# Narrowing the first layer's weights with Prelu, the first batch on small array tiles, and a new issue order

## The chip, the cores and the metric

The kernel runs on one core of a Trainium2 chip. Its metric is the device time of one execution in microseconds (us); lower is better. The profile shows one execution, taken by the hardware profiler. Engines are named as the profile names them: PE multiplies matrices (PEld loads its weights), DVE is the vector engine, ACT the scalar engine, POOL GpSimd, and SP issues the DMAs.

## What is computed

The inputs are float32, except that the four weight matrices reach the device as float64 words. A state attends to tokens and tokens to the state, in both directions; the two results, 2176 tokens of width 512, go through two feed-forward layers.

```python
B, H, S, Ns, D = (4, 8, 512, 32, 64)
a = softmax(scale * x @ state.T)          # per batch and head, over the 32 states
xread = a @ state
a2 = softmax(scale * state @ x.T)         # over the 512 tokens
sread = a2 @ x
x = concatenate([xread, sread])           # 4 * (512 + 32) tokens of 512
h = x @ w_in                              # 512 -> 1024
solu = h * softmax(h)
ln = (solu - mean(solu)) / sqrt(var(solu) + 1e-6) * g_ln
x = ln @ w_out                            # 1024 -> 512
h = x @ w2_in                             # 512 -> 2048
out = (h * tanh(softplus(h))) @ w2_out    # 2048 -> 512
```

## The kernel before

The 2176 tokens are 17 tiles of 128: four of each batch's 512 tokens, and tile 16 with the states of all four batches. Three stages follow each other, without a barrier between them.

**Start.** `s_load_w_in` and `s_load_w_out` (L275, L287) bring eight pieces each of the first layer's two weight matrices, 128x512 words of 64 bits, 512 KB apiece. `narrow` (L146) turns a piece into float32 with integer steps on the upper and the lower 32-bit word. It multiplies the upper word, read as a float32, by 2 to the power -112 (on ACT, L155, or on DVE, L153, as the flag string `W` says); it brings the lower word's top bits into place (ACT L158 or DVE L160, flag `B`); it shifts the upper word left by 3 and joins the two (DVE L165). The shift drops the sign. Either a second DVE instruction puts it back (L169), or, where flag `T` is 1, ACT has first written a float16 copy of the upper word over its upper half, which carries the sign to where the shift keeps it (L163). `s_gw` (L298) then splits each piece of `w_out`, scaled by `g_ln`, into a high part on ACT (L305) and a rest on DVE (L307).

The first batch's attention stands apart from that of the others. Its state is loaded as a block diagonal `bd_t` of 128x64 for each pair of heads; `s_tok_scores` (L321) and `s_tok_exp` (L329) compute the token side with the tokens on the partitions, `s_scores0` (L374) the state side with one matmul for a pair of heads, and `s_sw0` (L508) the product of state and `w_in`, one matmul for a pair and a half, which needs two of the eight pieces of `w_in` at a time. The other batches use `s_scores` and `s_sw` (L381, L518), eight matmuls each on tiles of 64 rows by 32 columns of the array, which write 32-partition strips of one PSUM tile; a half of `s_sw` needs four of the pieces of `w_in`. `s_back` (L451) weighs the tokens by the state's softmax, for the first batch with 64-column matmuls (L463), for the others with 32-column ones (L470).

**First layer.** For each tile `s_a0` (L529) makes `h` with matmuls of `aT` and `sw` (L548), `s_a1` (L553) the softmax and the normalisation (its first instruction is the maximum on DVE, L557), `s_turn` or `s_turn_far` the transpose, and `s_d` (L629) the product with `gw` (L640).

**Second layer.** Three passes over eight blocks (L868 on): `s_hp` (L884) multiplies with `w2_in` by a Strassen scheme of seven products, `s_post` combines them on DVE (the first of these combinations is L898), `s_act` applies Mish, `s_po` and `s_block` multiply with `w2_out`. The second layer's weights come and are narrowed (by the same `narrow`, with n of 16 and above) in the first pass.

`s_warm` (L240) issues matmuls on a constant tile, 26 at first and then groups of 4 where the flag string `R` has a 0; nobody reads their result.

The order of all of this is written out: each step is a generator, `ORDER` is a string of step numbers, two characters each, and the loop at L1174 advances the step named next by one `yield`. Each engine works in the order in which its instructions were so issued, and SP issues the DMAs in that order too. The flag strings choose the engine of single instructions.

## Time and profile before

| | us |
|---|---|
| median of 3 runs | 571.43 |
| lowest and highest | 570.12, 571.88 |
| the profiled execution's own time | 570.37 |
| its span in the profile | 568.6 |

In the span PE is busy for 98%, DVE for 89%, ACT for 63% and POOL for 9%. The busy share of an engine is a mean over stages with different limits, so the views below are cut by time. "Idle before" is the time for which an engine had nothing running just ahead of an instruction, with what ended it. A row with xN merges N instructions that follow each other.

### The profile page before, as it was taken

The numbers are of one execution on the slowest core, as the hardware profiler recorded it, in microseconds if no ns is written. First come the engines' busy times: TensorE is split into PE (matmuls) and PEld (weight loads), VectorE is DVE, ScalarE is ACT, GpSimd is POOL, SyncE is SP. The second block draws the span as 40 slices with busy tenths as digits, with TensorE's granted clock in tenths as the row PEclk, the third lists the DMA queues.
The fourth block names the chain that finished last, engine by engine and source line by source line (L and its number), as shares of the span: only waits on it lengthen the run. The fifth ranks groups of instructions, "written<-read, shape, count | busy, mean of one in ns | idle before, by whom it ended". The sixth has DMA issues, their size and how long they took to land. (4 is left out here: it accounts for less than half of the span.)

```text
span 568.6 us, 9811 instructions
## 1 busy us (share of the span) xinstructions
PE 555.6 (98%) x3513; PEld 491.9 (87%) x3513; DVE 504.5 (89%) x964; ACT 358.4 (63%) x660; POOL 52.2 (9%) x128
## 2 busy tenths in 40 slices
PE   9899999999999998999999999999999999999997
PEld 3434788899699997888988899999999999999996
DVE  5999989995779879999999998398999999998995
ACT  5998968565468646999979774643334635443340
POOL 0102212120023000000000000000000034000023
PEclk9999999999999999999999999999999999999999
DMA  8963225054217979999897979785796669897932
GB/s 307 415 229 113 75 88 185 27 174 124 75 75 221 300 254 325 316 329 343 310 336 297 355 277 382 273 302 203 249 338 235 253 222 345 282 342 279 318 125 94
DMA packets 50016, 139.19 MB, mean 245 GB/s; under 512 B 5680, under 2 KB 22704, under 8 KB 49968
## 3 DMA queue, kind: packets, MB, share of 16 engines
q1 hardware_dynamic: 49968, 138.57, 68.7%
q8 instruction: 28, 0.46, 0.3%
q14 instruction: 20, 0.16, 0.1%
HBM read 98.18 MB, written 40.37 MB: 244 GB/s over the span
## 5 line engine op out<-in xcount | busy, mean ns | idle before, releaser
L884 PE MATMUL hp<-xo,w2r 128*128 128x384 f32 (+1 forms) x504 | 93.8, 329 | 0.4 <-ACT w2r L705 0.3
L884 PEld LDWEIGHTS hp<-xo,w2r 128*128 128x128 f32 x504 | 84.5, 188 | 3.5 <-ACT w2r L705 0.7
L884 PE MATMUL hp<-xo,w2swh 128*128 128x384 f32 (+1 forms) x336 | 82.9, 330 | 3.1 <-DVE m L895 1.0
L640 PE MATMUL pm<-ln_l,gw_hi 128*128 128x256 f32 (+1 forms) x256 | 76.8, 300 | 0.0
L640 PE MATMUL pm<-ln_h,gw_hi 128*128 128x256 f32 (+1 forms) x256 | 75.0, 293 | 0.0
L640 PE MATMUL pm<-ln_h,gw_lo 128*128 128x256 f32 (+1 forms) x256 | 74.5, 291 | 0.0
L996 DVE TENSOR_TENSOR acc<-po,acc 128x384 f32<-128x384 f32 (+1 forms) x136 | 69.0, 521 | 2.6 <-PE po L991 1.6
L884 PEld LDWEIGHTS hp<-xo,w2swh 128*128 128x128 f32 x336 | 59.1, 188 | 6.4 <-DVE m L895 1.3
L925 ACT ACTIVATE gh<-c 128x384 fp32r<-128x384 f32 (+1 forms) x57 | 29.3, 516 | 51.8 <-DVE c L906 44.9
L884 PE MATMUL hp<-xo,w2swl 128*128 128x384 f32 (+1 forms) x168 | 55.1, 328 | 0.0
L963 ACT CAST qh<-t 128x384 fp32r<-128x384 f32 (+1 forms) x60 | 28.9, 489 | 37.1 <-DVE t L955 22.5
L640 PEld LDWEIGHTS pm<-ln_l,gw_hi 128*128 128x128 f32 x256 | 48.2, 188 | 3.0 <-issue 1.6
L640 PEld LDWEIGHTS pm<-ln_h,gw_hi 128*128 128x128 f32 x256 | 48.2, 188 | 1.2 <-issue 0.7
L640 PEld LDWEIGHTS pm<-ln_h,gw_lo 128*128 128x128 f32 x256 | 48.7, 190 | 0.0
L906 DVE TENSOR_TENSOR c<-hp,u 128x384 f32<-128x384 f32 (+1 forms) x72 | 38.1, 531 | 10.7 <-PE hp L884 9.9
L548 PE MATMUL ph<-swh,aT 128*128 128x512 f32 x128 | 44.1, 449 | 0.4 <-ACT ph L566 0.4
L989 PE MATMUL po<-ql,w2oh 128*128 128x384 f32 (+1 forms) x120 | 39.3, 328 | 0.2 <-DVE acc L996 0.2
L990 PE MATMUL po<-qh,w2oh 128*128 128x384 f32 (+1 forms) x120 | 38.7, 323 | 0.0
L991 PE MATMUL po<-qh,w2ol 128*128 128x384 f32 (+1 forms) x120 | 38.7, 323 | 0.0
L965 DVE TENSOR_TENSOR ql<-t,qh 128x384 fp32r<-128x384 f32 (+1 forms) x60 | 32.0, 544 | 0.6 <-ACT qh L963 0.2
L548 PEld LDWEIGHTS ph<-swh,aT 128*128 128x128 f32 x128 | 22.6, 189 | 10.7 <-issue 4.3
L884 PEld LDWEIGHTS hp<-xo,w2swl 128*128 128x128 f32 x168 | 31.5, 188 | 0.0
(454 smaller groups left out, 1346.5 us busy)
## 6 DMA issues: line engine op xcount, KB each, us to landing
w2r<-ki SPq DMA_DIRECT2D x16, 768.0 KB, 5.8
w2ol<-ko SPq DMA_DIRECT2D x15, 768.0 KB, 6.1
w2oh<-ko SPq DMA_DIRECT2D x15, 768.0 KB, 6.7
w<-in_w2i SPq DMA_DIRECT2D x16, 512.0 KB, 5.7
w2swh<-ki SPq DMA_DIRECT2D x8, 896.0 KB, 6.2
w2swl<-ki SPq DMA_DIRECT2D x8, 896.0 KB, 7.3
td<-tt SPq DMA_DIRECT2D x12, 512.0 KB, 2.7
ln_l<-td SPq DMA_DIRECT2D x48, 128.0 KB, 3.1
```

The costliest lines, as they stand in the source:

```text
L548: nc.tensor.matmul(out=ph[:, hf * 512:(hf + 1) * 512], lhsT=a_[:, c * P:(c + 1) * P], rhs=w_[:, q, hf * 512:(hf + 1) * 512], start=q == 0 ...
L640: nc.tensor.matmul(out=pm[:, :n], lhsT=w_[:, k, m * P:(m + 1) * P], rhs=l_[:, c0:c0 + 4 * len(blk), k, :], start=k == 0 and j == 0, stop=k ...
L884: nc.tensor.matmul(out=r, lhsT=w_[:, 0, k * P:(k + 1) * P], rhs=x_[:, k, :n], start=s in (0, 1, 3, 4) and cnt == 0, stop=cnt == 5, skip_gr ...
L906: nc.vector.tensor_tensor(out=c, in0=bank[ps, fp, s], in1=u, op=ALU.add)
L925: nc.scalar.activation(out=gh, in_=src, func=AF.Mish)
L963: nc.scalar.copy(out=hi, in_=src)
L965: on('V', ((ps - 1) * NFP + fp) * 4 + int(name[1]) - 1).tensor_tensor(out=lo, in0=src, in1=f32(hi), op=ALU.subtract)
L989: nc.tensor.matmul(out=r, lhsT=wh[:, a, c], rhs=x[1], start=first or not held, stop=False)
L990: nc.tensor.matmul(out=r, lhsT=wh[:, a, c], rhs=x[0], start=False, stop=False)
L991: nc.tensor.matmul(out=r, lhsT=wl[:, a, c], rhs=x[0], start=False, stop=last or not held)
L996: on.tensor_tensor(out=o, in0=x, in1=y, op=ALU.add)
```

## The change

`narrow` handles n below 16, the first layer's sixteen pieces, in a way of its own. The upper word goes through one ACT instruction, Prelu with a scale of 2 to the power -112 and a slope of 2 to the power 32 for negative values. A negative value comes out with 32 added to its exponent, and the shift by 3 moves that exponent bit into the sign's place. The lower word is treated as before, and one DVE instruction joins the two. The second DVE instruction, the float16 copy and the choice of the engine for the multiplication (flag `W`) are gone for these pieces.

The first batch's `s_scores0` and `s_sw0` are removed; `s_scores(0)` and `s_sw(0, hf)` take their place, and `s_back(0, q)` uses the code of the other batches. `s_tok_scores` keeps its matmuls and writes their 64 columns as two runs of 32.

`ORDER` is a new string (3144 entries in place of 3182), and nine flag strings have other digits. The groups on the constant tile fall from seven to six.

```diff
 REBIAS = 2.0 ** -112
+NEGATIVE = 2.0 ** 32
...
-    B="00011111001011100001000001101110",
+    B="11011011000010000111010010101000",
...
-    "AAAABKBKATBIBIBQBQBSBSBMBMBCBCBABAARARBLBLATAUAUBLAWAWBJBJBLBJBOBOBRBJBRANANBWBRA-A-BTBWADADBXBTA0A0BRAJAJBNBXBN"
+    "AAAAAUAUBQBQBMBMBABAARARBIBIBKBKBSBSATAWAWBRBRBRAYAYBNBNBNAaAaBBASASBcBBBBANANBCBCBJBJAPAPBJA2A2BLBLAQAQBLABABA0"
...
     low, high = src[..., 0], src[..., 1]
-    signs = eng('T', n, False, True)
-    if eng('I', n, False, True):
-        nc.gpsimd.tensor_scalar(out=f32(high), in0=f32(high), scalar1=REBIAS, scalar2=None, op0=ALU.mult)
+    sided = n < 16
+    signs = not sided and eng('T', n, False, True)
+    if sided:
+
+        nc.scalar.activation(out=f32(high), in_=f32(high), func=AF.Prelu, scale=REBIAS, alpha=NEGATIVE)
     elif eng('W', n, False, True):
...
-    nc.vector.scalar_tensor_tensor(out=words(dst) if signs else low, in0=high, scalar=3, in1=low,
+    last = sided or signs
+    nc.vector.scalar_tensor_tensor(out=words(dst) if last else low, in0=high, scalar=3, in1=low,
                                    op0=ALU.logical_shift_left, op1=ALU.bitwise_or)
-    if not signs:
+    if not last:
         yield
...
-        toks[b] = ph = ps_h.tile([P, 4, 2, 2, 64], F32, tag="ph", name="ph")
+        toks[b] = ph = ps_h.tile([P, 4, 2, NPAIR, NS], F32, tag="ph", name="ph")
...
-    def s_scores0(q):
-        sts[0, q] = st = ps_m.tile([P, S], F32, tag="mm", name="st")
-        for j in range(2):
-            p = 2 * q + j
-            nc.tensor.matmul(out=st[of_head(j), :], lhsT=bd_t[:, p, :], rhs=xT_t[0, p], start=True, stop=True)
-            yield
...
-    def s_sw0(q, j, hf):
-        ph = once(("sw0", q), lambda: ps_h.tile([P, FF1], F32, tag="ph", name="ph"))
-        p = 2 * q + j
-        nc.tensor.matmul(out=ph[of_head(j), hf * 512:(hf + 1) * 512], lhsT=bd_t[:, p, :],
-                         rhs=w_in_half(2 * p + hf), start=True, stop=True)
-        yield
...
-        plan(s_scores0, q)
-        for j in range(2):
-            for hf in range(2):
-                plan(s_sw0, q, j, hf)
-        plan(s_sw0_split, q)
+    plan(s_scores, 0)
+    for hf in range(2):
+        plan(s_sw, 0, hf)
```

What the new order does at three places is shown in the words of the two programs' orders. The names are those of tiles: `wo` and `wi` hold pieces of `w_out` and `w_in` as they came, `xT_t` the transposed tokens, `bd_t` and `st_t` the state in its two layouts, `e` a softmax's numerators, `ex` the token side's weights, `spare` the constant tile. In the changed kernel L154 is the Prelu, L163 is what L160 was, L169 what L165 was, L292 and L280 the loads of `w_out` and `w_in`, L268 that of `xT_t`, L251 the constant tile, L329 and L383 the scores, L494 `s_sw`, L520 `s_a0`.

The first place is SP's queue at the very start. Before:

```order
L288 DMA wo_163<-in_w_out 128x1024
L256 DMA g_t<-in_g_ln 128x8
L288 DMA wo_163<-in_w_out 128x1024
L288 DMA wo_167<-in_w_out 128x1024 x2
L288 DMA wo_170<-in_w_out 128x1024
L276 DMA wi_172<-in_w_in 128x1024 x2
L252 DMA bd_t<-in_bd 128x256
L264 DMA xT_t<-in_xT 128x512 x2
```

and after:

```order
L268 DMA xT_t<-in_xT 128x512
L292 DMA wo_165<-in_w_out 128x1024
L292 DMA wo_167<-in_w_out 128x1024
L280 DMA wi_169<-in_w_in 128x1024
L256 DMA bd_t<-in_bd 128x256
L292 DMA wo_172<-in_w_out 128x1024 x2
L292 DMA wo_165<-in_w_out 128x1024
L260 DMA g_t<-in_g_ln 128x8
L268 DMA xT_t<-in_xT 128x512 x3
```

One piece of `xT_t` moved from behind seven pieces of weights to the front of the queue, one piece of `w_in` and `bd_t` moved ahead of the third piece of `w_out`, and the other three pieces of `xT_t` follow the first five of `w_out`.

The second place is DVE's queue while it works on these first pieces, from the first instruction on a piece. Before:

```order
L160 TENSOR_SCALAR wo_163<-wo_163 128x512
L258 TENSOR_SCALAR g_t<-g_t 128x8
L165 SCALAR_TENSOR_TENSOR wo_163<-wo_163 128x512
L153 TENSOR_SCALAR wo_163<-wo_163 128x512
L169 SCALAR_TENSOR_TENSOR wo_163<-wo_163 128x512
L165 SCALAR_TENSOR_TENSOR wo_163<-wo_163 128x512
L169 SCALAR_TENSOR_TENSOR wo_163<-wo_163 128x512
L165 SCALAR_TENSOR_TENSOR wo_167<-wo_167 128x512
L307 SCALAR_TENSOR_TENSOR gw_lo<-wo_163,g_t,gw_hi 128x512
```

and after:

```order
L163 TENSOR_SCALAR wo_165<-wo_165 128x512
L169 SCALAR_TENSOR_TENSOR wo_165<-wo_165 128x512
L169 SCALAR_TENSOR_TENSOR wo_167<-wo_167 128x512
L169 SCALAR_TENSOR_TENSOR w_in_t<-wi_169 128x512
L163 TENSOR_SCALAR wo_172<-wo_172 128x512
L169 SCALAR_TENSOR_TENSOR wo_172<-wo_172 128x512
L163 TENSOR_SCALAR wo_172<-wo_172 128x512
L169 SCALAR_TENSOR_TENSOR wo_172<-wo_172 128x512
L163 TENSOR_SCALAR wo_165<-wo_165 128x512
L262 TENSOR_SCALAR g_t<-g_t 128x8
L169 SCALAR_TENSOR_TENSOR wo_165<-wo_165 128x512
L311 SCALAR_TENSOR_TENSOR gw_lo<-wo_172,g_t,gw_hi 128x512 x2
```

The second instruction on each piece is gone, and six pieces are joined before the first `gw_lo` in place of three.

The third place is PE's queue between the last groups on the constant tile and the first `s_a0` (weight loads left out). Before, all of the constant tile's groups come first, and then:

```order
L378 MATMUL st<-xT_t,bd_t 64x512 x2
L325 MATMUL ph<-bd_t,xT_t 128x64 x8
L511 MATMUL ph<-w_in_t,bd_t 64x512
L511 MATMUL ph<-w_in_230,bd_t 64x512
L325 MATMUL ph<-bd_t,xT_t 128x64 x8
L352 MATMUL tr<-ident,e_299 128x128 x4
L511 MATMUL ph<-w_in_t,bd_t 64x512
L378 MATMUL st<-xT_t,bd_t 64x512 x2
L511 MATMUL ph<-w_in_t,bd_t 64x512
L463 MATMUL sr<-xn_t,a_338 64x128 x8
L511 MATMUL ph<-w_in_t,bd_t 64x512 x4
```

and after, where two groups on the constant tile stand right ahead of the first row:

```order
L356 MATMUL tr<-ident,e_306 128x128 x4
L494 MATMUL ph<-w_in_t,st_t 32x512 x6
L494 MATMUL ph<-w_in_272,st_t 32x512 x2
L494 MATMUL ph<-w_in_t,st_t 32x512 x6
L494 MATMUL ph<-w_in_272,st_t 32x512 x2
L356 MATMUL tr<-ident,ex 128x128 x4
L356 MATMUL tr<-ident,e_352 128x128 x4
L494 MATMUL ph<-w_in_t,st_t 32x512 x8
L356 MATMUL tr<-ident,ex 128x128 x4
L383 MATMUL st<-xT_t,st_t 32x512 x8
L494 MATMUL ph<-w_in_t,st_t 32x512 x8
L520 MATMUL ph<-swh,aT 128x512 x2
```

The scores of the first batch (L329 and L383) now stand ahead of these rows, the weighing of the first batch's tokens behind them, and the matmuls with the block diagonal are gone.

## Rows read from the trace of the kernel before

**Rows 1.** Windows: from:to, length, busy us (instructions), PEclk, DMA share, GB/s.
```profile
20.00:40.00 20.00, 17.23 (x131) 7.89 (x131) 19.86 (x34) 19.95 (x33) 1.44 (x4) 1.00 0.81 312
40.00:60.00 20.00, 19.65 (x138) 9.26 (x138) 19.37 (x36) 17.37 (x34) 5.88 (x21) 1.00 0.32 106
60.00:80.00 20.00, 20.00 (x189) 16.66 (x185) 18.79 (x32) 15.85 (x30) 4.06 (x13) 1.00 0.22 73
```
**Rows 2.** Windows of 4 us in the start: the same columns, PE first.
```profile
0.00:4.00 4.00, 2.96 (x7) 1.04 (x8) 0.17 (x1) 1.28 (x1) 0.72 (x7) 1.00 0.46 138
4.00:8.00 4.00, 4.00 (x19) 1.83 (x18) 1.84 (x5) 1.32 (x2) 0.00 (x0) 1.00 0.94 310
8.00:12.00 4.00, 4.00 (x21) 1.77 (x19) 3.59 (x7) 3.27 (x7) 0.00 (x0) 1.00 1.02 414
24.00:28.00 4.00, 2.25 (x14) 0.91 (x13) 4.00 (x6) 4.00 (x8) 0.29 (x1) 1.00 1.03 412
```
**Rows 3.** Waits of DVE from 0 to 80 us: total us, times, longest.
```profile
DVE wo L160 <- DMA wo<-in_w_out: 3.1, 1, 3.1
DVE wo L153 <- DMA wo<-in_w_out: 1.9, 1, 1.9
```
**Rows 4.** Timeline of all engines: start, us, engine, line, what.
```profile
13.03 1.28 DVE L165 SCALAR_TENSOR_TENSOR wo<-wo 128x512 uint32<-128x512 uint32 x2
14.92 1.63 PE L378 MATMUL st<-xT_t,bd_t 128*64 128x512 f32 x4 [0.38 <-DMA xT_t<-in_xT]
18.23 0.74 DVE L307 SCALAR_TENSOR_TENSOR gw_lo<-wo,g_t,gw_hi 128x512 fp32r<-128x512 f32 x1
27.12 2.58 ACT L163 CAST wi<-wi 128x512 f16<-128x512 f32 x2
29.39 0.79 ACT L155 ACTIVATE wi<-wi 128x512 f32<-128x512 f32 x1
34.47 1.08 PE L522 MATMUL ph<-w_in_t,st_t 64*32 64x512 f32 x16
```
**Rows 5.** Groups by form on DVE, 4 to 44 us: xcount, busy us, mean ns.
```profile
L307 DVE SCALAR_TENSOR_TENSOR gw_lo<-wo,g_t,gw_hi 128x512 fp32r<-128x512 f32 x8 | 5.9, 743 | 0.0
L169 DVE SCALAR_TENSOR_TENSOR wo<-wo 128x512 uint32<-128x512 uint32 x7 | 4.9, 701 | 0.1
L169 DVE SCALAR_TENSOR_TENSOR w_in_t<-wi 128x512 uint32<-128x512 uint32 x4 | 2.8, 693 | 0.1
L160 DVE TENSOR_SCALAR wo<-wo 128x512 uint32<-128x512 uint32 x4 | 1.8, 450 | 3.1 <-DMA wo<-in_w_out 3.1
L153 DVE TENSOR_SCALAR wo<-wo 128x512 f32<-128x512 f32 x2 | 0.9, 428 | 1.9 <-DMA wo<-in_w_out 1.9
```
**Rows 6.** Groups by form on ACT, 4 to 44 us.
```profile
L305 ACT ACTIVATE gw_hi<-wo,g_t 128x512 fp32r<-128x512 f32 x8 | 6.2, 780 | 0.0
L155 ACT ACTIVATE wi<-wi 128x512 f32<-128x512 f32 x8 | 5.4, 682 | 0.0
L163 ACT CAST wi<-wi 128x512 f16<-128x512 f32 x4 | 5.3, 1386 | 0.0
```
**Rows 7.** Groups by form on PE, 14 to 40 us.
```profile
L511 PE MATMUL ph<-w_in_t,bd_t 128*64 128x512 f32 x14 | 6.9, 616 | 2.6 <-DVE ex L336 1.8 <-DVE w_in_t L169 0.8
L378 PE MATMUL st<-xT_t,bd_t 128*64 128x512 f32 x8 | 3.5, 608 | 0.4 <-DMA xT_t<-in_xT 0.4
```
**Rows 8.** Timeline: the first tile's matmuls, the maxima of the first and fifth tile.
```profile
39.84 1.98 PE L548 MATMUL ph<-swh,aT 128*128 128x512 f32 x4
44.24 1.21 DVE L557 TENSOR_REDUCE lnsm<-ph 128x1 f32<-128x1024 f32 x1
66.17 1.21 DVE L557 TENSOR_REDUCE lnsm<-ph 128x1 f32<-128x1024 f32 x1
```
**Rows 9.** Timeline of PE's weight loads on the constant tile, early and later.
```profile
4.00 0.15 PEld L247 LDWEIGHTS <-spare 128*128 128x128 bf16 x1 [0.27 <-issue]
4.43 9.61 PEld L247 LDWEIGHTS <-spare 128*128 128x128 bf16 x45 [0.28 <-issue]
```

More of the change, by code (lines that the diff above doesn't have):

```diff
@@ L321, in s_tok_scores @@
     def s_tok_scores(b):
-        toks[b] = ph = ps_h.tile([P, 4, 2, 2, 64], F32, tag="ph", name="ph")
+        toks[b] = ph = ps_h.tile([P, 4, 2, NPAIR, NS], F32, tag="ph", name="ph")
         for p in range(NPAIR):
             for c in range(4):
-                nc.tensor.matmul(out=ph[:, c, p // 2, p % 2, :], lhsT=xT_t[b, p][:, c * P:(c + 1) * P],
-                                 rhs=bd_t[:, p, :], start=True, stop=True)
+                nc.tensor.matmul(out=ph[:, c, :, p, :], lhsT=xT_t[b, p][:, c * P:(c + 1) * P],
+                                 rhs=bd_t[:, p, :].rearrange("p (j n) -> p j n", n=NS), start=True, stop=True)
             yield
     def s_tok_exp(b):
-        ph = toks[b].rearrange("p c q j (h n) -> p (c q j h) n", n=NS)
+        ph = toks[b].rearrange("p c j q n -> p (c j q) n")
         mx = sm_p.tile([P, 32], F32, tag="mx4", name="mx4", bufs=1)
@@ L458, in s_back @@
         tok = slice(b * NS, (b + 1) * NS)
-        if b == 0:
-            sr = ps_m.tile([P, P], F32, tag="mm", name="sr")
-            for k in range(4):
-                for j in range(2):
-                    nc.tensor.matmul(out=sr[of_head(j), :], lhsT=a2[:, k, of_head(j)], rhs=xn_t[b, 2 * q + j][:, k, :],
-                                     start=k == 0, stop=k == 3)
-        else:
-            sr = once(("sr", b), lambda: ps_m.tile([P, P], F32, tag="mm", name="sr"))
-            for k in range(4):
-                for p in range(NPAIR):
-                    r = slice(NS * p, NS * p + NS)
-                    nc.tensor.matmul(out=sr[r, of_head(q)], lhsT=a2[:, k, r], rhs=xn_t[b, p][:, k, of_head(q)],
-                                     start=k == 0, stop=k == 3)
+        sr = once(("sr", b), lambda: ps_m.tile([P, P], F32, tag="mm", name="sr"))
+        for k in range(4):
+            for p in range(NPAIR):
+                r = slice(NS * p, NS * p + NS)
+                nc.tensor.matmul(out=sr[r, of_head(q)], lhsT=a2[:, k, r], rhs=xn_t[b, p][:, k, of_head(q)],
+                                 start=k == 0, stop=k == 3)
         yield
-        if b and q == 0:
+        if q == 0:
             return
         srs = at_w.tile([P, P], F32, tag="srs", name="srs", bufs=1)
-        if b:
-            nc.scalar.activation(out=srs[:, of_head(0)], in_=sr[:, of_head(0)], func=AF.Copy, scale=a2s[b, 0][1])
-            nc.scalar.activation(out=srs[:, of_head(1)], in_=sr[:, of_head(1)], func=AF.Copy, scale=s2)
-        else:
-            nc.scalar.activation(out=srs, in_=sr, func=AF.Copy, scale=s2)
+        nc.scalar.activation(out=srs[:, of_head(0)], in_=sr[:, of_head(0)], func=AF.Copy, scale=a2s[b, 0][1])
+        nc.scalar.activation(out=srs[:, of_head(1)], in_=sr[:, of_head(1)], func=AF.Copy, scale=s2)
         yield
```

140 lines of the change are left out of this document (66 added, 74 removed).

## The prediction

> **What bounds the kernel now.** I read the windows first, in steps of 20 us. From 60 us on PE is busy for the whole of each window, and DVE for 18.79 of 20 [rows 1]: what comes later is PE's, and it moves as a block with the moment at which the tiles of the first layer start to flow. From 20 to 40 us it is otherwise. DVE has 19.86 of 20 and ACT 19.95, while PE has 17.23 [rows 1]; in the middle of it, from 24 to 28 us, DVE and ACT are full and PE has 2.25 of 4 [rows 2]. So DVE and ACT are what limits the start. DVE stays with them to the fifth tile: from 40 to 60 us it still has 19.37 of 20 [rows 1].
>
> Before that the loads set the pace. The DMA moves 138 GB/s in the first four us, 310 in the next, and 412 to 414 from then on, where its engines are full (1.02 to 1.03) [rows 2]. DVE waits 3.1 and 1.9 us for pieces of `w_out` [rows 3], and after the second of them it has no long wait. The two points to measure from are the maxima (L557) of the first tile, at 44.24 us, and of the fifth, at 66.17 us [rows 8]: DVE gets there with a queue that never emptied, so work taken out ahead of them comes off in full, unless something else is late.
>
> **The change, part by part.** First the price of an instruction in a full queue. Two L165 that follow each other take 1.28 us together, so with 0.69 for the second the first costs 0.60 [rows 4]. L169 has the same shape and the same mean, 0.69 to 0.70 [rows 5]. L160 and L153 cost 0.45 and 0.43 each by their means [rows 5], about 0.34 from start to start by the same subtraction. On ACT two casts L163 start at 27.12 and the next instruction at 29.39, so one costs 1.13 [rows 4], and L155 some 0.57 against its mean of 0.68 [rows 6].
>
> DVE loses eleven L169 (seven for `wo`, four for `wi` [rows 5]): 11 x 0.60 = 6.6 us. It loses two L153 and gains two L160, which cancel. Counted over the two orders, 65 DVE instructions stand ahead of the first tile's maximum before and 53 after, and their prices sum to 36.5 and 29.8 us, 6.7 less. Ahead of the fifth tile's maximum it is 99 and 87, and 7.3 us less, since there the new order has also put one reduction of 0.6 behind. ACT loses five casts, 5 x 1.13 = 5.6 us. It gains two multiplications that DVE did and loses two shifts, which cancel too, so ACT is relieved by nearly as much as DVE.
>
> The Prelu is in no row. Its nearest row is L155, an ACTIVATE on the same words with the same scale, 0.68 [rows 6]; the dearest ACT instruction on 128x512 is the cast, 1.39 [rows 6]; nothing excludes that it is a little cheaper than L155. I take L155's price, since both read and write the same words in place, and L305, another form with a per-partition scale and another output, is only 0.1 dearer [rows 6]. The Trainium skill (ScalarE: Activation LUTs, What ACT_TABLE_LOAD costs) says that an ACTIVATE runs at one element per cycle whatever its function; by it the sum would be the one I make, and no run here shows a Prelu yet. The order has as many table loads as before, two, so Prelu brings none.
>
> PE loses much in the start: eight matmuls L511, 6.9 us of busy time for seven of them, and four L378, 3.5 us [rows 7]. In their place come `s_sw(0)` and `s_scores(0)`, three groups like the one of L522 that takes 1.08 us [rows 4]. That is some 10 us against 3.3. I count none of it as a gain: PE has room in that stage, and it waits for DVE there (2.6 us before L511 [rows 7]). What covers it is DVE's and ACT's queue; without that cover it would be worth the whole difference. It does mean that PE is not next late. From the fifth tile's first matmul on both orders leave PE the same matmuls to within 0.1 us, so PE passes on what DVE brings there.
>
> The loads are next late. Their volume is the same, but the order is not. Ahead of and with the sixth piece of `w_out` or `w_in` that DVE needs before its first run of `gw_lo`, the new queue has five pieces of `w_out` and one of `w_in` at 0.52 MB, one `xT_t` at 0.26 and `bd_t` at 0.13: 3.5 MB. By the windows 1.8 MB have come at 8 us, and the other 1.7 at 0.414 MB per us take to 12.2 us [rows 2]. The same count puts the first `xT_t` of before (4.1 MB) at 13.5, and its matmul, which waited for it, began at 14.92 [rows 4]; so a landing is 1.4 us behind the count, and the piece is there at 13.6. Then come one Prelu (0.57), five L305 on ACT at 0.67 from start to start, and a last L307, 0.66: DVE ends the run at 18.2 us, with 9.1 us of work done, 9.1 us idle. Before, DVE ends its L307 of 18.23 us at 18.9 [rows 4] with 12.3 us of work done, 6.6 idle. The new order therefore begins 2.5 us worse, and has 7.3 us less to do.
>
> The sum: 7.3 - 2.5 = 4.8 us earlier at the fifth tile. The bounds of the load term are 0 (the pieces come as early as they did) and 2.5 + 3.1 = 5.6 (one more wait like the longest of DVE [rows 3]); I take 2.5, since it is counted from bytes and from a landing that the trace shows. The rest of the new order, some 2900 entries for the later stages, has the same matmuls and DMAs in other places; I price it at nothing, because PE is full there, with 1.5 us either way in the range, about the PE time that single late buffers cost in the start [rows 7].
>
> **The rivals.** *The loads are not late.* For it: the pieces are issued without a wait, and the queue's order is only a guess at the order of landing. Against: DMA engines full from 8 us on [rows 2]. Then all of 7.3 us is kept.
>
> *The loads are later still.* One more wait of 3.1 us [rows 3] leaves 1.7 us. For it: the first piece for DVE now stands behind `xT_t`, in the four us in which the DMA is slowest, 138 GB/s [rows 2]. Against: 0.26 MB are less than 1 us at 310 GB/s.
>
> *PE's clock falls.* The weight loads on the constant tile are 0.43 us apart up to 4.43 us and then 45 of them fill 9.61 us, 0.21 apart [rows 9]: these are the two levels, 1.2 and 2.4 GHz. Before, the granted clock held at 1.00 through the four us in which PE was busy for 2.25 [rows 2]. The new order leaves between the constant tile's last group (about 19 us) and the first softmax numerators (about 23 us, after DVE's maximum, POOL and ACT) nothing for PE, and then until the first `s_a0` only eight groups of 0.45 to 1.08 us. At 1.2 GHz their 7 us become 14, in a stretch of some 10 to 14 us; about half of the excess would delay the first tile, so 3 us of the 4.8 go. The Trainium skill (TensorE: Matmul & The Clock Gate, Part 1: The HAM clock gate) says that the array goes back to half rate when it has been idle; by that rule the time is this rival's. The trace so far shows no fall at all, with the smallest share 2.25 of 4, so I give it little.
>
> *Prelu costs what the cast costs.* This one ends slower. At 1.13 us in place of 0.57 sixteen of them add 9.0 us to ACT ahead of the first tile, against 5.6 saved: 3.4 us more on an engine with 19.95 of 20 [rows 1]. It decides from 0.35 us more per Prelu (5.6/16) on. For it: the cast shows that not every instruction on these words runs at L155's price. Against: the cast writes half-words at a stride, the Prelu does not.
>
> **How the numbers follow.** All sums go by the profiled execution: span 568.6, own time 570.37, so 1.8 us lie outside the span; the median of 571.43 is 1.06 above it, and I keep both distances. Forecast: 568.6 - 4.8 = 563.8 in the span, 565.6 for such an execution, 566.6 as a median; chance 0.55, own range 565 to 568. Loads not late: 571.4 - 7.3 = 564.1, chance 0.17. Loads later still: 571.4 - 1.7 = 569.7, chance 0.12. Clock falls: 571.4 - 1.8 = 569.6, chance 0.10. Prelu dear: 571.4 + 3.4 = 574.8, chance 0.06.
>
> About 0.3%, 1.7 us, is what a measurement of this kernel can tell from no change, so faster means below 569.7. The first two cases lie there, and half of the third and fourth: 0.55 + 0.17 + 0.11 = 0.83. The other half is the same, 0.11, and slower is the last, 0.06. The range goes from 562.5 (the second case with the order's 1.5 us) to 570.0, which leaves out the last case, a third of the third and fourth, and a little at the lower end.
>
> **What would show it.** Right: no L169 for the first layer; DVE and ACT full from 18 us on; the first tile's maximum near 40 us and the fifth's near 61.4; windows from 65 us on like those of before, 4.8 us earlier; DVE's waits for loads some 2.5 us longer in total. Wrong: ACT waiting less than DVE with Prelu rows near 1.1 us; a granted clock under 1.00 between 19 and 35 us; the fifth tile early but the span not, which would mean that the order of the later stages takes it back.

## The result, and the profile after

The changed kernel takes 563.81 us (median of 4 runs, 563.49 to 564.55); the kernel before 570.77 (569.61 to 571.88). The ratio is 0.988, 95% interval 0.9855 to 0.9905: 7.0 us faster, where 4.8 were forecast. The forecast of 566.6 lies 2.8 us above, the range held the time. The profiled execution of after has a span of 562.1 us, before it was 568.6.

Five more lines of the new file are needed: the shift on ACT is L161, `gw_hi` and `gw_lo` are L309 and L311, the token maximum (the first instruction of `s_tok_exp`) L336 and the tile's maximum L529. Windows of after, with the columns of [rows 1]:

```profile
20.00:40.00 20.00, 14.51 (x143) 5.84 (x144) 19.48 (x34) 18.42 (x33) 1.88 (x7) 1.00 0.78 299
40.00:60.00 20.00, 20.00 (x188) 12.10 (x187) 19.55 (x37) 17.89 (x33) 6.13 (x23) 1.00 0.48 159
60.00:80.00 20.00, 20.00 (x211) 16.29 (x210) 17.86 (x29) 14.19 (x24) 4.37 (x14) 1.00 0.14 54
```

DVE is as full from 20 to 40 us as it was (19.48 against 19.86), but with less work per tile: PE is at 20.00 of 20 from 40 us on, where before had 19.65. The groups by form on DVE, 4 to 44 us, answer to [rows 5]:

```profile
L169 DVE SCALAR_TENSOR_TENSOR wo<-wo 128x512 uint32<-128x512 uint32 x8 | 5.5, 692 | 2.6 <-ACT wo L161 1.8 <-ACT wo L154 0.5
L169 DVE SCALAR_TENSOR_TENSOR w_in_t<-wi 128x512 uint32<-128x512 uint32 x7 | 4.6, 688 | 0.8 <-ACT wi L161 0.7
...
```

and those on ACT to [rows 6]:

```profile
...
L154 ACT ACTIVATE wo<-wo 128x512 f32<-128x512 f32 x8 | 5.5, 692 | 6.1 <-DMA wo<-in_w_out 6.1
L154 ACT ACTIVATE wi<-wi 128x512 f32<-128x512 f32 x8 | 5.4, 693 | 0.1
```

One join for each piece is left (the sixteenth is written to `w_in`, in a group of its own). The Prelu's mean is 0.69 us, against 0.68 for the Copy in [rows 6] and 1.39 for the cast: the rival with a dear Prelu is dead. The timeline of ACT (start us, us, engine, line) with the Prelu of the sixth piece and two that follow each other:

```profile
12.78 0.68 ACT L154 ACTIVATE wo<-wo 128x512 f32<-128x512 f32 x1 [0.62 <-DMA wo<-in_w_out]
...
22.42 1.24 ACT L154 ACTIVATE wi<-wi 128x512 f32<-128x512 f32 x2
```

PE's timeline with the first tile's matmuls, and DVE's with the first run of five `gw_lo`, the token maximum and the maxima of the first and the fifth tile, for [rows 8]:

```profile
34.09 1.98 PE L520 MATMUL ph<-swh,aT 128*128 128x512 f32 x4
```

```profile
14.15 3.41 DVE L311 SCALAR_TENSOR_TENSOR gw_lo<-wo,g_t,gw_hi 128x512 fp32r<-128x512 f32 x5
17.47 1.22 DVE L336 TENSOR_REDUCE mx<-ph 128x32 f32<-128x1024 f32 x1
...
39.02 1.21 DVE L529 TENSOR_REDUCE lnsm<-ph 128x1 f32<-128x1024 f32 x1
...
60.98 1.21 DVE L529 TENSOR_REDUCE lnsm<-ph 128x1 f32<-128x1024 f32 x1
```

The maximum of the first tile comes 5.2 us earlier than in [rows 8] (39.02, was 44.24), that of the fifth 5.2 us too (60.98, was 66.17). Behind that the lead shrinks to 4.7 us at the second layer's first matmul (210.3, was 215.0) and grows to 6.5 at the end of the span: 1.8 us come in the second layer. Waits of DVE in after, 0 to 80 us (total, times, longest), for [rows 3], and the longest of PE:

```profile
DVE wo L163 <- DMA wo<-in_w_out: 4.3, 1, 4.3
DVE wo L169 <- ACT wo L161: 1.8, 1, 1.8
```

```profile
PE tr L356 <- ACT e L442: 3.3, 1, 3.3
```

DVE waits once for a piece (4.3 us; before 3.1 and 1.9) and then for a shift on ACT, whose Prelu had itself waited 1.3 us for its piece. Over the whole way to the fifth tile's maximum the windows of before and then of after are (DVE is the third busy time):

```profile
0.00:66.17 66.17, 61.63 (x385) 31.06 (x386) 58.76 (x102) 56.89 (x97) 9.72 (x37) 1.00 0.66 245
```

```profile
0.00:60.98 60.98, 52.81 (x436) 27.77 (x437) 51.68 (x90) 50.38 (x87) 8.73 (x37) 1.00 0.72 266
```

DVE is busy for 7.1 us less and idle for 9.3 us in place of 7.4, so 1.9 more: together the 5.2 us.

The marks of all the kernels run stand here together, from their profiled executions; the medians of before beside them were 570.5 to 570.9 us. The token maximum L336 stands in the new order right behind the five `gw_lo`, so its start says when the start's first part is over; the next column is the way from there to the first tile's maximum.

| kernel | token maximum | from it to the first tile's | first tile's maximum | second layer's first matmul | from there to the span's end | median us |
|---|---|---|---|---|---|---|
| before | - | - | 44.2 | 215.0 | 353.6 | 570.77 |
| after | 17.5 | 21.55 | 39.0 | 210.3 | 351.8 | 563.81 |
| e1_narrow_old_order | - | - | 41.4 | 212.6 | 353.9 | 568.37 |
| e2_new_order_old_narrow | 19.9 | 29.92 | 49.8 | 220.5 | 351.8 | 574.55 |
| e2w_longer_warm | 18.9 | 29.93 | 48.9 | 220.5 | 352.1 | 574.63 |
| e3_join_twice_early | 20.2 | 21.56 | 41.8 | 212.9 | 351.9 | 566.50 |
| e4_join_twice_late | 17.8 | 25.22 | 43.0 | 213.7 | 351.8 | 567.30 |
| e5_block_diagonal | 16.9 | 21.94 | 38.8 | 212.7 | 351.8 | 566.92 |
| e9b_x_behind_six | 20.7 | 21.57 | 42.3 | 214.3 | 352.4 | 568.26 |
| e9c_x_behind_six_scores_later | 17.1 | 21.54 | 38.7 | 209.8 | 351.8 | 563.75 |
| e11_old_second_order | 17.3 | 22.27 | 39.5 | 211.7 | 351.1 | 564.15 |
| e7_before_new_m | - | - | 44.4 | 215.4 | 353.1 | 570.82 |
| e12_before_second_earlier | - | - | 44.4 | 215.7 | 356.7 | 573.84 |
| e13_new_second_order | - | - | 44.0 | 216.8 | 357.3 | 576.43 |

From the first tile's maximum to the second layer it is 170.7 to 172.1 us in all of them but two (172.8 in e13, 173.9 in e5), whichever of the two orders the first layer has. So the prediction's first reading holds, to within that spread of about 1.4 us: what is gained at the first tile arrives at the end of the first layer.

### The profile page after: what moved, and what is told of

The parts are those of the page before. It is cut to its first block, busy times and chain, and to the rows that moved or that the text cites. A ratio compares the mean times of both kernels' runs of the same rounds, so it can differ in the third digit from the quotient of the medians.

```text
span 562.1 us, 9891 instructions
## 1 busy us (share of the span) xinstructions
PE 547.0 (97%) x3564; PEld 488.3 (87%) x3564; DVE 498.8 (89%) x952; ACT 349.6 (62%) x648; POOL 54.8 (10%) x131
## 4 chain that ended last, share of the span: by engine, by line
PE 80%; DVE 7%; ACT 5%; DMA 4%; issue 2%; SPq 1%; ACTq 0%; DVEq 0%
PE hp L856 26%; PE pm L612 13%; PE ph L520 8%; PE po L961 6%; PE po L962 6%; PE po L963 6%; PE po L912 3%; PE po L913 3%; PE po L911 3%; DMA ln_l<-td 2%; PE po L1029 1%; PE ph L507 1%; ACT w L166 1%; DMA bd_t<-in_bd 1%; PE ph L494 1%
## 5 line engine op out<-in xcount | busy, mean ns | idle before, releaser
L935 ACT CAST qh<-t 128x384 fp32r<-128x384 f32 (+1 forms) x60 | 28.8, 489 | 35.5 <-DVE t L927 20.2
L520 PE MATMUL ph<-swh,aT 128*128 128x512 f32 x128 | 45.8, 454 | 0.0
L961 PE MATMUL po<-ql,w2oh 128*128 128x384 f32 (+1 forms) x120 | 39.5, 329 | 1.0 <-DVE acc L968 1.0
L963 PE MATMUL po<-qh,w2ol 128*128 128x384 f32 (+1 forms) x120 | 38.8, 323 | 0.0
L962 PE MATMUL po<-qh,w2oh 128*128 128x384 f32 (+1 forms) x120 | 38.7, 323 | 0.0
L166 ACT CAST w<-w 128x512 f16<-128x512 f32 x22 | 30.9, 1405 | 7.4 <-DVE w L163 5.8
L520 PEld LDWEIGHTS ph<-swh,aT 128*128 128x128 f32 x128 | 22.1, 189 | 11.5 <-issue 6.0
```

The source lines that it names most:

```text
L166: nc.scalar.copy(out=src.bitcast(F16)[..., 1], in_=f32(high))
L520: nc.tensor.matmul(out=ph[:, hf * 512:(hf + 1) * 512], lhsT=a_[:, c * P:(c + 1) * P], rhs=w_[:, q, hf * 512:(hf + 1) * 512], start=q == 0 ...
L935: nc.scalar.copy(out=hi, in_=src)
L961: nc.tensor.matmul(out=r, lhsT=wh[:, a, c], rhs=x[1], start=first or not held, stop=False)
L962: nc.tensor.matmul(out=r, lhsT=wh[:, a, c], rhs=x[0], start=False, stop=False)
L963: nc.tensor.matmul(out=r, lhsT=wl[:, a, c], rhs=x[0], start=False, stop=last or not held)
```

## The experiments: narrowing and order apart

**The narrowing alone, in the old order.**

```diff
--- before
+    sided = n < 16
+    signs = not sided and eng('T', n, False, True)
+    if sided:
+        nc.scalar.activation(out=f32(high), in_=f32(high), func=AF.Prelu, scale=REBIAS, alpha=NEGATIVE)
...
+    if sided:
+        yield
+    last = sided or signs
-    nc.vector.scalar_tensor_tensor(out=words(dst) if signs else low, ...
+    nc.vector.scalar_tensor_tensor(out=words(dst) if last else low, ...
```

> The kernel before, with one edit: the first layer's sixteen pieces are narrowed with Prelu and one join, each instruction at the place where the old order had it (the join at the place of the last of the old ones). The vector engine loses the 11 sign joins at 0.60 us and two multiplications at 0.33, 7.3 us; the scalar engine loses 5 casts at 1.13 and gains two passes at 0.57, -4.5 us. Theory A (the two engines bound the first stage by their counts of work, and the issue order only has to be no worse): most of the 7.3 us arrive, but an order made for other work loses some: 564.5 to 567.5 against 570.8 before. Theory B (the new order is what gives the time; less work in the old order only turns into waits): 569.5 to 571. Theory C (both engines freed and nothing else was late): 563.5.

Measured: 568.37 us, ratio to before 0.9954 (0.9941 to 0.9967), 2.4 us faster. It lies between A and B: of 7.3 us taken from DVE, 2.8 arrive at the first tile. The first 20 us of before and then of this run (DVE is the third busy time):

```profile
0.00:20.00 20.00, 18.58 (x78) 8.33 (x78) 13.53 (x24) 13.88 (x21) 1.06 (x8) 1.00 0.90 338
```

```profile
0.00:20.00 20.00, 18.96 (x78) 8.53 (x78) 10.27 (x19) 14.36 (x23) 1.33 (x8) 1.00 0.91 341
```

DVE works 3.3 us less there and stands 3.3 us longer. Its waits in this run say for what:

```profile
DVE wo L162 <- DMA wo<-in_w_out: 3.3, 1, 3.3
DVE wo L170 <- ACT wo L160: 3.1, 1, 3.1
DVE gw_lo L312 <- ACT gw_hi L310: 1.5, 2, 1.3
```

For the loads as before (3.1 us in [rows 3]), and now for ACT's shifts and products, which the old order has where DVE used to be busy with sign joins.

**The order and the small tiles, with the old narrowing.**

```diff
--- after
-    sided = n < 16
+    sided = False
...
-    B="1101101100001000...  T="1100100110000010...  W="1000000101100011...
+    B="0001111100101110...  T="1100100110000000...  W="0000000001100000...
```

(the last two instructions of a piece are issued one behind the other, since the new order has three steps for a piece).

> The kernel after, with one edit: the first layer's pieces narrowed as before (five casts, eleven sign joins, the old choice of engines for the shifts and multiplications), the last two instructions of a piece issued one behind the other. The vector engine gets 7.3 us of work back. Six of the eleven sign joins then lie in the stretch in which the vector engine waits for the loads (3.0 us of idle time between its first join and the five differences that end at 17.5 us in the trace of after). Theory A (vector and scalar engine bound the stage outside that stretch): between 3.7 and 7.3 us slower than after, 567.5 to 571. Theory B (the order and the small tiles give the time, the narrowing little): 564 to 565.5.

Measured: 574.55 us, ratio 1.0064 (1.005 to 1.0078): 10.7 us slower than after and 3.8 slower than before, beyond the 571 of A. The token maximum is 2.4 us later than in after, and the way from it to the first tile 8.4 us longer. On that way (windows of after and then of e2) DVE is busy for 4.2 us more, with five sign joins and one multiplication, and idle for 4.2 us more:

```profile
17.47:39.02 21.55, 15.34 (x149) 6.04 (x149) 21.03 (x36) 20.18 (x35) 1.88 (x7) 1.00 0.85 327
```

```profile
19.87:49.80 29.93, 18.69 (x142) 6.77 (x143) 25.19 (x43) 24.93 (x38) 1.85 (x7) 0.77 0.52 201
```

The idle time is in DVE's waits for the casts (L166). Ahead of the first two of these ACT itself stood, for DVE's sign join (L175):

```profile
DVE w_in_t L170 <- ACT wi L166: 2.2, 2, 1.4
DVE wo L170 <- ACT wo L166: 1.5, 1, 1.5
```

```profile
33.61 0.77 ACT L311 ACTIVATE gw_hi<-wo,g_t 128x512 fp32r<-128x512 f32 x1 [2.72 <-DVE wo L175]
```

So the two queues cross: ACT waits 2.7 us for DVE's late sign join, two casts (34.29 and 36.37 us) stand behind that on ACT, and DVE waits for them in turn. The casts cost more than their own time there, because the new order has no other work of DVE between a cast and its join. The parts do not add: narrowing alone 2.4 us faster, the rest alone 3.8 slower, both together 7.0 faster. The order is worth what it is for this work, and the work for this order.

## The experiments: what a join costs, early and late

```diff
--- after
     last = sided or signs
+    if n in (14, 12, 6, 10, 11, 15):        # e3; e4 has (2, 3, 5, 9, 13)
+        nc.vector.scalar_tensor_tensor(out=words(dst), in0=high, scalar=3, in1=low, ...
```

> The kernel after, with the join of the first six weight pieces issued twice (the second writes the same values again): 6 x 0.60 = 3.6 us more on the vector engine, all of it ahead of the five differences that begin at 14.15 us, in the stretch where the vector engine stood 3.0 us between its first join (6.0 us) and there, waiting for pieces or for the scalar engine. Theory A (the loads cover part of it): set one behind the other with the waits that the trace of after has, the five differences begin at 16.45 in place of 14.15 us, 2.3 us slower, 566.1. Theory B (every join costs its 0.60 wherever it lies): 567.4. Theory C (until the loads are in, joins are free): within 0.5 us of after, 563.8 to 564.3.

Measured: 566.50 us, 2.7 above after (theory A: 566.1). The token maximum comes at 20.20 us in place of 17.47, 2.7 later: up to there DVE is busy for 4.0 us more and idle for 1.3 less. The way from there is the same to 0.01 us.

> The kernel after, with the join issued twice for five of the pieces that come later (behind 17.5 us): 5 x 0.60 = 3.0 us more on the vector engine, where it was busy 19.5 of 20 us. Theory A (the vector engine bounds the stage there): 3.0 us slower, 566.8, and the maximum of the first tile at 42.0 in place of 39.0 us. Theory B (TensorE or the scalar engine bounds it, the vector engine only looks full): at most 1 us slower, 564.8.

Measured: 567.30 us, 3.5 above after. The token maximum is at 17.80, the first tile 25.22 us behind it in place of 21.55: 3.7 us where 3.0 were expected. The 0.7 on top are DVE's own. A join and its repetition on the same piece start 0.73 us apart, not 0.60:

```profile
24.11 0.69 DVE L170 SCALAR_TENSOR_TENSOR w_in_t<-wi 128x512 uint32<-128x512 uint32 x1
24.84 0.69 DVE L172 SCALAR_TENSOR_TENSOR w_in_t<-wi 128x512 uint32<-128x512 uint32 x1
25.45 0.68 DVE L170 SCALAR_TENSOR_TENSOR w_in_t<-wi 128x512 uint32<-128x512 uint32 x1
```

Five of these are the 3.7 us, and DVE has the same one wait as in after on that way (0.3 us). So theory A holds: DVE bounds the way to the first tile, though PE waited 3.5 us for these joins and its granted clock was 0.57 in the window from 28 to 32 us.

## The experiments: TensorE's part and its clock

**The block-diagonal first batch in the new order.**

```diff
--- after
+            if b == 0:
+                q, j = divmod(p, 2)
+                nc.tensor.matmul(out=sts[0, q][of_head(j), :], lhsT=bd_t[:, p, :], rhs=xT_t[0, p], start=True, stop=True)
+                continue
...
+            if b == 0:
+                q, j = divmod(p, 2)
+                nc.tensor.matmul(out=ph[of_head(j), q, :], lhsT=bd_t[:, p, :], rhs=w_in_half(2 * p + hf),
+                                 start=True, stop=True)
+                continue
```

(token scores and the way back of the first batch as before, too).

> The kernel after, with one edit: the first batch's scores and weights are computed as before, with the block-diagonal state on 128 rows (four matmuls for the scores, eight for the weights, 0.86 us each in the trace of before) in place of three groups of small tiles at 1.08 us; the order stays as it is. TensorE gets about 7 us of work back between 15 and 45 us, where it was busy 14.5 of 20 us (20 to 40 us) in the trace of after. Theory A (TensorE is not what bounds the start; the prediction counted its gain at nothing): within 0.7 us of after, 563.3 to 564.5. Theory B (TensorE is late from the first ln tile on, so its work there counts whole): 7 us slower, 570.8. In between (the weights of the first batch end later and the first product with them waits): 1.5 to 3.5 us slower.

Measured: 566.92 us, ratio 0.9934 (0.9919 to 0.9948), 3.1 above after: the last of the three cases. The way from the token maximum to the first tile's is only 0.4 us longer. The second tile's maximum is 27.95 us behind the token maximum in place of 26.62: 1.3 us lost, and by the marks of the first layer's matmuls it is 1.3 to 1.8 up to 189 us. There another 1.4 us go in this profile, 3.0 in all at the second layer's first matmul: PE waits 1.4 us for a copy on ACT (`raw_d`), which stood behind two waits of ACT for DMAs, 1.5 and 1.1 us. Whether that second part belongs to the edit is open. PE is slack up to the first tile and tight from about the second on.

**The clock.** In e2 PE stood 6.4 us for the first softmax numerators and the granted clock fell. Windows of e2:

```profile
20.00:24.00 4.00, 0.00 (x0) 0.00 (x0) 3.84 (x6) 3.85 (x5) 0.00 (x0) 0.76 1.03 418
24.00:28.00 4.00, 2.70 (x8) 0.90 (x8) 3.69 (x7) 4.00 (x9) 0.77 (x3) 0.50 1.03 411
28.00:32.00 4.00, 2.18 (x24) 0.66 (x28) 3.93 (x9) 2.89 (x6) 0.45 (x1) 0.50 1.00 368
```

0.50 is the lower of the two levels, 1.2 GHz. The next kernel fills that stop.

```diff
--- e2_new_order_old_narrow
-        for _ in range(4 if k else 26):
+        for _ in range(16 if k in (3, 9) else 4 if k else 26):
```

> The run with the old narrowing in the new order, once more, with one edit: the two filler groups that TensorE runs behind the first batch's scores are 16 matmuls long instead of 4. In the trace of that run they began at 17.0 us, TensorE then stood 6.4 us, and the granted clock was 0.5 from 22.1 to 35.7 us. 24 more at 0.21 us fill 5.1 of the 6.4 us. Theory A (that stop costs the clock, and the clock costs time): the clock stays at 1.0 there and the first tile's maximum, at 49.8 us, comes 2 to 3.5 us earlier, 571 to 572.5 against 574.6; what is left above after is then the vector engine's 7.3 us. Theory B (the vector and the scalar engine alone make it late, a slower TensorE is hidden): the clock stays up and the time stays within 0.7 us of 574.6.

Measured: 574.63 us, the same as without the fillers (574.55): theory B. The clock stayed at 1.00 through the window from 24 to 28 us, and the way from the token maximum to the first tile is 29.93 us, with half clock there 29.92. The clock fell later in this run (0.78 from 28 to 32 us, 0.63 and 0.51 from 36 to 44), where e2 has 1.00 from 36 us on. So the end alone could hide a gain that was lost again; a mark between settles it: the first of the two casts above starts 14.4 us behind the token maximum in e2 (34.29) and 14.5 in e2w (33.38), so the half clock that e2 alone had before 30 us cost nothing up to there either. Another pair says the same of that stretch. In the window from 24 to 28 us after and e9c have

```profile
24.00:28.00 4.00, 3.03 (x37) 1.18 (x36) 3.97 (x9) 4.00 (x9) 0.23 (x1) 1.00 1.03 413
```

```profile
24.00:28.00 4.00, 3.24 (x30) 0.66 (x28) 3.96 (x9) 4.00 (x9) 0.29 (x1) 0.50 1.02 412
```

and both reach the first tile 21.5 us behind the token maximum, as e3 does, also at 0.50 there. In e11, which has the same first layer as after, word for word, the clock fell later. Its windows from 28 to 36 us are

```profile
28.00:32.00 4.00, 2.37 (x21) 0.81 (x22) 3.72 (x8) 4.00 (x7) 0.33 (x1) 0.84 1.05 389
32.00:36.00 4.00, 4.00 (x38) 1.50 (x38) 3.74 (x7) 3.51 (x7) 0.21 (x1) 0.73 0.21 57
```

Its first tile comes 0.7 us later behind the token maximum than in after, the second 1.5 (28.09 against 26.62). Three rows of e11 say whose these are:

```profile
27.29 0.69 ACT L442 ACTIVATE e<-st,m 128x512 f32<-128x512 f32 x1
32.26 1.23 DVE L488 TENSOR_TENSOR swl<-ph,swh 128x1024 fp32r<-128x1024 f32 x1 [0.51 <-ACT swh L486]
45.34 1.22 DVE L529 TENSOR_REDUCE lnsm<-ph 128x1 f32<-128x1024 f32 x1 [0.86 <-PE ph L520]
```

The ACT row stands 10.04 us behind the token maximum, in after 9.40 (26.87): ACT was 0.6 us late already then, with the granted clock at 1.00 up to 30 us, and DVE waited for ACT at 32.26. That is the first tile's 0.7, and not the clock's; what held ACT is not shown. Only the other 0.8 us, at the second tile, are waited for on PE, behind the stretch at half clock. So the clock's price was nothing up to the first tile and at most 0.8 us at the second, where PE is tight. This last number rests on one pair of executions; no edit tested it.

## The experiments: the loads

**The first x tile behind the sixth weight piece.** `AU` is its load in the table of the order.

```diff
--- after
-    "AAAAAUAUBQBQBMBMBABAARARBIBIBKBKBSBSATAWAW...
+    "AAAABQBQBMBMBABAARARBIBIBKBKBSBSAUAUATAWAW...
```

> The kernel after, with the load of the first x tile (256 KB, which stood ahead of all weights) moved behind the sixth weight piece. At the 366 to 402 GB/s of the first 15 us of after that is 0.65 to 0.7 us, by which each of the first six pieces lands earlier. Theory A (the sixth piece's landing sets when the vector engine's run of five differences ends, as the prediction's load term has it): the run ends 0.5 to 0.7 us earlier and the time is 563.1 to 563.3. Theory B (the first token scores, which need that x tile, or the scalar engine are as late as the pieces): within 0.2 us of after, or slower.

Measured: 568.26 us, 4.5 above after. The first half of theory A seems to be there, and more than its 0.5 to 0.7 us: the five differences begin at 13.01 us in place of 14.15. (The next run shows how far such a start scatters.) Then DVE waits for the token scores. PE's timeline in this run:

```profile
11.82 1.25 PE L329 MATMUL ph<-bd_t,xT_t 128*128 128x64 f32 x8 [2.69 <-DMA xT_t<-in_xT]
12.87 5.16 PE L251 MATMUL warm<-spare 128*128 128x512 bf16 x16
17.87 2.79 PE L329 MATMUL ph<-bd_t,xT_t 128*128 128x64 f32 x24
```

and DVE:

```profile
20.69 1.22 DVE L336 TENSOR_REDUCE mx<-ph 128x32 f32<-128x1024 f32 x1 [4.28 <-PE ph L329]
```

The first four score matmuls stand ahead of sixteen fillers on PE. PE waits 2.7 us for the x tile and begins 2.8 us later than in after (11.82, was 9.03). The granted clock is 0.57 from 12 to 16 us, the fillers take 5.16 us in place of 3.62, and so the remaining scores come 4.3 us later than in after, 2.8 of it by the x tile and 1.5 by the clock. A filler that holds the clock is on the path when it is queued ahead of something that DVE wants.

**The same, with those four matmuls (`Bc`) behind the fillers.**

```diff
--- e9b_x_behind_six
-    ...BNBNBNAaAaBBASASBcBBBBANAN...
+    ...BNBNBNAaAaBBASASBBBBANAN...      (Bc now ahead of the next Bc)
```

> The run with the first x tile behind the sixth weight piece, with one more edit: the first four matmuls of the token scores, which stood ahead of four filler groups on TensorE, are issued behind them. In that run the vector engine's five differences ended 1.1 us earlier than in after (16.3 in place of 17.5 us), but TensorE stood 2.7 us for the x tile at 9 us, its granted clock was 0.5 from 12.6 to 16.0, the fillers took 5.2 us in place of 3.6, and the vector engine waited 4.3 us for the scores. Theory A (the load term is real, and what took it back was TensorE's stop): the scores end near 16.4 us, the clock stays up, and the time is 0.7 to 1.2 us below after, 562.6 to 563.1. Theory B (the scalar engine, or the later weight pieces, are as late): within 0.4 us of after.

Measured: 563.75 us, ratio 0.9883 (0.986 to 0.9905), the same as after. The stop is gone, the token maximum is at 17.12, 0.35 us earlier than in after. With the same six loads as e9b in front, the five differences now begin at 13.81, not at 13.01. That shows what one profile can tell of the loads: e4 and e11 have after's code to that point, e5 all of it but the first batch's scores, and their token maxima are at 17.80, 16.88 and 17.25 against 17.47. The start of the kernel moves by 0.9 us from one profiled execution to the next, more than this edit gives.

## The experiments: the 1.8 us of the second layer

From 200 to 230 us PE waited 2.8 us in before, in after 1.2. The waits of before, and then of after:

```profile
PE hp L884 <- DVE m L895: 1.0, 1, 1.0
PE hp L884 <- DVE u L901: 0.9, 1, 0.9
PE hp L884 <- ACT a__2552 L918: 0.7, 1, 0.7
```

```profile
PE hp L856 <- ACT a__2554 L890: 1.2, 1, 1.2
```

**The copy m on ACT**, as in after:

```diff
--- before
-    M="110000000001101000010000",
+    M="000000000001101000010000",
```

> The kernel before, with one edit: the copies that open the second layer's first two blocks go to the scalar engine, as in after, instead of the vector engine. In the trace of before TensorE stood 2.7 us between 215 and 230 us, 1.0 of it for that copy and 1.1 for the sums behind it; after has 1.2 us there in all. Theory A (the flag is what gave the 1.5 us that came behind the first layer): 1.0 to 1.6 us faster than before, 569.2 to 569.8. Theory B (the new order of the second layer's start gave it, the flag alone nothing): within 0.3 us of before, or slower by up to 1 us because the scalar engine is busy with the first weights there.

Measured: 570.82 us, ratio 0.9995 (0.9983 to 1.0007). The choice of engine alone gives nothing.

**The old order behind the end of the first layer**, with the old choices of engine there; the table of the order is cut behind the last call of `s_d` and goes on with the old one's steps that are left.

```diff
--- after
-    B="...0111010010101000"  M="000000001100000001000000"  S="101111"  T="...1000111111111111"  W="...0011101010101100"
+    B="...0001000001101110"  M="110000000001101000010000"  S="101000"  T="...0000111111111111"  W="...0001100001001101"
```

> The kernel after up to the last matmul of the first layer; from there on all steps in the order of the kernel before, with the second layer's choices of engine as before. In the traces the first layer ends 4.6 us earlier in after than in before, the last matmul of the second layer's first product 5.8 us earlier, and the span is 6.5 us shorter. Theory A (the 1.9 us that came behind the first layer are the new order of the second layer): 1.5 to 2.2 us slower than after, 565.3 to 566.0. Theory B (they come from the first layer's different end, by what is then ready): within 0.4 us of after, 563.4 to 564.2.

Measured: 564.15 us, ratio 0.9889 (0.9873 to 0.9905), 0.3 above after: theory B. From the second layer's first matmul on it even takes 351.1 us against 351.8. So the gain is decided before that point.

**The splits of the second block earlier, in the old order.**

```diff
--- before (names of steps)
+ (from further behind) load64(0,2)#2..4, split_in(1,0)#0, split_in(1,1)#0, keep_in(1,0)#0, split_in(1,0)#1, split_in(1,1)#1, keep_in(1,1)#0
  split_osum(1,0)#0
```

> The kernel before, with one edit in its order: the narrowing of the third piece of the second layer's first weights, the two splits of its second block and their two stores are issued ahead of the sums' splits of that block, about ten steps earlier, as after has them (there they stand ahead of the first layer's last matmuls). In before TensorE takes 13.2 us from the second layer's first matmul to the first one that reads those splits, in after 11.0, and 2.8 us of it stood in before. The run with the old order behind the first layer's end took no longer there (11.1 us). Theory A (how far these splits are when the first layer ends is what gives the 1.8 us): 11 to 11.5 us there and 1.4 to 2.0 us faster than before, 568.5 to 569.1. Theory B (something else that stands ahead of the first layer's end): within 0.5 us of before.

Measured: 573.84 us, ratio 1.0051 (1.0031 to 1.0071): slower, and not what either theory said. The stores `keep_in` came along and stand in SP's queue ahead of the next weight loads, waiting for the splits. SP's issues of those loads in before, in after and in this run:

```profile
213.73 0.38 SPq L664 DMA_DIRECT2D w<-in_w2i  x1
215.03 0.42 SPq L664 DMA_DIRECT2D w<-in_w2i  x1
```

```profile
204.88 0.42 SPq L636 DMA_DIRECT2D w<-in_w2i  x1
206.35 0.47 SPq L636 DMA_DIRECT2D w<-in_w2i  x1
```

```profile
217.25 0.38 SPq L664 DMA_DIRECT2D w<-in_w2i  x1
218.55 0.41 SPq L664 DMA_DIRECT2D w<-in_w2i  x1
```

Against the second layer's first matmul (215.0, 210.3 and 215.7 us) the first of the two loads is issued 1.2 us ahead in before, 5.5 ahead in after and 1.5 behind in this run. From that matmul to the 43rd of the layer, the first that reads the next weights, it is 13.2, 10.9 and 16.5 us.

**The new order behind the end of the old first layer.** The mirror image of e11, cut in the same way.

> The kernel before up to the last matmul of the first layer; from there on all steps in the order of after, with the second layer's choices of engine as in after: the mirror image of the run with the old order behind that point. From the second layer's first matmul to the end of the span before takes 353.6 us, after 351.8, and the new first layer with the old order behind it took 351.1. Theory A (what has been issued ahead of that point gives the 1.8 us, the order behind it nothing): 353 to 354 us and 570.2 to 571.4 in all. Theory B (the new order behind that point can give them as well): 351 to 352 us and 568.3 to 569.3 in all.

Measured: 576.43 us, ratio 1.0102 (1.0086 to 1.0119), 357.3 us from the second layer's first matmul on. Neither number was right, and B is excluded. Here the load is issued 0.8 us ahead, and the new order, which is written for 5.5, waits for it. PE stands 3.4 us for the copy `m` on ACT, and the copy stands behind a shift that waited for the load:

```profile
221.27 0.70 ACT L158 ACTIVATE w<-w 128x512 uint32<-128x512 uint32 x1 [1.57 <-DMA w<-in_w2i]
221.86 0.47 ACT L895 COPY m<-hp 128x384 f32<-128x384 f32 x1
```

The same shift waits 1.7 us for the load in before, and the copy `a__2552` of PE's third wait stands behind it on ACT; of the other two one stands behind DVE's busy queue, the other behind a wait of DVE (0.6 us) for the store `ko`. In e13 the granted clock is 0.74 from 220 to 225 us, behind that stop, so a part of its 16.0 us below is the clock's. Over all runs: where the load is 5.4 to 5.5 us ahead (after, e2, e2w, e3, e4, e5, e9b, e9c, e11) the 42 matmuls take 10.9 to 11.8 us, with 1.2 to 1.6 ahead (before, e1, e7) 12.7 to 13.2, and in e13 and e12 16.0 and 16.5. That the lead of these loads gives the 1.8 us fits all of them and e12's step in the other direction. It is not shown by itself: no run moved the loads alone, since they wait for one of three weight buffers.

## Why the prediction was right, and where it was not

**DVE bounds the start: right.** e3 and e4 price a repeated join at 0.45 us ahead of the token maximum (2.7 by 6), where a wait takes in a part, and at 0.73 behind it (3.7 by 5), the whole of the distance between two joins on one piece; the sum had 0.60, the distance between joins on different pieces. The count of 7.3 us less work stands (7.1 by the windows to the fifth tile). By the narrowing alone (e1) only 2.8 of it arrive, so "a queue that never emptied" was true of the old order only with its old work: there the freed time went into waits for loads and ACT. The prediction forecast the sum of both, and that came out.

**The load term: mechanism right, size 1.9 instead of 2.5.** The sixth piece was to land at 13.6 us, its Prelu began at 12.78; DVE was to end the five `gw_lo` at 18.2 and ended them at 17.47. Up to the fifth tile DVE was idle for 1.9 us more than before: 7.1 - 1.9 = 5.2, as measured. That these are the loads is read from DVE's waits; the edit that moved a load (e9c) gave less than the scatter. The 0.6 between 2.5 and 1.9 are less than the 0.9 by which the start of the same code scatters, so the term could not have been had more closely from one trace.

**ACT: price of the Prelu right, the casts' place in the queue left out.** The two Prelus of 22.42 us take 1.24 together, so one costs 0.55 from start to start; the forecast said 0.57. The Trainium skill (ScalarE: Activation LUTs, What ACT_TABLE_LOAD costs) says that an ACTIVATE takes one element per cycle whatever its function; the Prelu agrees, at 0.69 for 128x512 against 0.68 for the Copy of [rows 6]; the cast on the same shape does not, at 1.39. The five casts were counted as ACT's time. In e2 DVE also waited 3.7 us for three of them, two of which had stood behind ACT's own wait for DVE. What ACT's time alone is worth was not tried.

**PE's gain at nothing: right for the first tile, wrong behind it.** With the block-diagonal matmuls the first tile is 0.4 us later behind the token maximum, the second 1.3. The argument looked at the stage up to the first tile, where PE waits for DVE; behind it PE is busy for the whole of 40 to 60 us in after.

**The clock's rival: a fall did come, its price did not.** In after's profile PE stood 3.3 us and the granted clock stayed at 1.00. In e9c it fell after a stop of 2.9 us, in e3 after 6.0. The Trainium skill (TensorE: Matmul & The Clock Gate, Part 1: The HAM clock gate) says that the array goes back to half rate after idling, and e3 and e9c agree (0.50 from 24 to 28 us); after's own 3.3 us show no fall. The rival's step that failed is "about half of the excess would delay the first tile": in e2, e3, e4 and e9c none of it did.

**The rest of the new order at nothing, 1.5 either way: the step that failed most.** It gave 1.8 us in the second layer, less 0.5 on the way through the first. "PE is full there" was read from windows of the first layer; at the second layer's start before has PE waits of 2.8 us, which were in the trace and not in the sum. e11 shows that this came from what was issued ahead of the second layer, not from the order behind it. Of the 2.8 us between forecast and result 1.3 are this term and 0.4 the fifth tile. The rest is the 1.06 that the forecast added from the profiled execution to the median: after's median lies 0.10 below its profiled execution (563.91). (By its own terms, 564.1 - 1.5, the range's lower end is 562.6, not 562.5.)

## What to carry to other kernels

Work taken from a full engine comes off in full only when the order around it is made for the new work: the same edit gave 2.4 us in the old order and 10.7 in the new one, so an edit should be judged with its order, and each part only by undoing it in the final one. Read each stage's start for waits, not only its windows: the 1.8 us at the second layer's start, which go with weight loads issued 4 us earlier, are as much as three joins. On an engine with slack, slower work costs little or nothing, whether it comes from the block-diagonal matmuls (0.4 us at the first tile) or from half the clock; find the point where the slack ends before pricing either. And before a late mark is put down to a clock that fell, look whether another queue was late ahead of the fall, as ACT was in e11.

## What the runs showed of the chip that was not expected

Half of TensorE's granted clock for some 7 us (e9c, e3) and for 13 us (e2) cost nothing measurable at the first tile, and a fall between 30 and 35 us, with the same code as after, at most 0.8 us at the second (e11). Whether the clock falls is not the same from one execution to the next: after's own profile shows no fall between 20 and 36 us, e11 with the same first layer does. Two joins on DVE that work on the same piece start 0.73 us apart, two on different pieces 0.60 (e4). And two profiled executions of the same loads put the token maximum up to 0.9 us apart.
